# A fifth pair of hidden chunks by seven block products, two more tiles on written lists, and the output products chained in their banks

## The chip, the core and the metric

The kernel runs on one core of a Trainium2 chip. Its engines are TensorE (PE in the profile; its weight loads are the row PEld), VectorE (DVE), ScalarE (ACT), GpSimd (POOL) and SyncE (SP), which here only issues DMAs. Each engine takes its own instructions in order and waits for the others by semaphores. The metric is the device time of one execution in microseconds (us); a profiled execution gives the trace.

## What is computed

Blockwise causal attention over 8 batches of 8 heads, 576 positions and 64 dimensions, then a gated feed-forward layer over the 4608 tokens:

```python
batch, n_heads, seq, head_dim = (8, 8, 576, 64)
n_tokens, d_model, d_ff = (4608, 512, 1536)

scores = scale * np.matmul(q, k.transpose(0, 1, 3, 2))
mask = block_i >= block_j                    # blocks of 64 positions
scores = np.where(mask, scores, -1000000000.0)
attn = np.exp(scores - np.max(scores, axis=-1, keepdims=True))
attn = attn / (np.sum(attn, axis=-1, keepdims=True) + 1e-09)
x = np.matmul(attn, v).transpose(0, 2, 1, 3).reshape(B * S, H * D)

gate = np.maximum(x @ w_gate, 0.0)
val = x @ w_val
return (gate * val @ w_out).astype(np.float32)
```

## The kernel before

**Tiles.** The tokens are worked through in nine tiles of 512. Tile j (0 to 7) holds the first 512 positions of batch j; tile 8 holds the 64 last positions of all batches. While PE works on the feed-forward of tile j it also does the attention of batch j+1, so that the transposed attention output `xT` of the next tile is there when it begins. Tiles 7 and 8 have no attention beside them.

**Feed-forward of a tile.** The 1536 hidden columns are 12 chunks of 128. A plain chunk is eight matmuls that move 512 columns each (four for the gate, `g`, four for the value, `v`), a relu on ACT (`r`) and a product on DVE (`h`). The out-projection multiplies the 12 chunks of `hT` by `w_out`: plainly it is 48 matmuls of 512 columns.

**Seven block products.** Where two chunks are taken as a pair, gate and value of 256 hidden columns are made out of seven block products in place of eight (Strassen's scheme in Winograd's form): each product is four matmuls of 256 columns (L1348, in `times`), over sums of blocks of `xT` (`X1` to `X7`, L1154) and of the weights (`U..`, L950). The products land in three PSUM banks y, z and m. In the lists, `p15` is a matmul step of pair 1, product 5; the letters after it are the evacuation of a pair: `a`, `b`, `l` copy banks to SBUF on ACT (L1371, L1374, L1389), `r` is a relu on ACT, `s`, `m`, `y`, `z` are f32 additions (L1377, L1382, L1393, L1396; `s` on POOL where `ON_POOL` says so), `H` and `L` are the products that make the two halves of `hT` (L1401, L1415). Pair n is chunks 2n and 2n+1. Tiles 3 to 6 take four pairs so (1, 2, 3, 5) and four chunks plainly (0, 1, 8, 9), tiles 7 and 8 all six pairs, tiles 0 to 2 none.

**The out-projection by seven products** (L1033, in `seven_products`) is 84 matmuls of 256 columns over sums of `hT` (`s....`, L992 on DVE) and of `w_out` (`weight_sums`, `weight_differences`; the latter change `w_out` in place). Tiles 2 to 8 use it, tiles 0 and 1 are plain (L1265). `M5` is a step of two matmuls of product 5. Products 3 and 5 share bank y, 4 and 2 bank z; 1, 6 and 7 have a bank each. `oa`, `oy`, `oz` are ACT copies out of y and z (L1085, L1092, L1095); `ob`, `om`, `oc`, `od`, `o6`, `o7` are f32 additions (L1080; `od` on POOL). `S0` to `S3` store a quarter of the tile.

**What sets the order.** Tiles 3 to 8 follow lists (`ORDER_3_6`, `ORDER_7`, `ORDER_8`): each word emits a step, and each engine's queue holds its own instructions in the order of the words. Tiles 0 to 2 come from a generator of matmul steps (`ffn_gen`), into which the other work is put at places in a table (`AT`). Which of two or three PSUM banks a tile uses is written out too (`SLOTS`, `PAIR_BANK`). Attention in a list: `A` computes scores, `E` their exponentials (ACT, L616 and L623), `C` zeroes masked corners in `attnT` (L1526, eight memsets in a tile on DVE), `V` multiplies by v (L759, L773), `N` normalises (DVE), `T` transposes by DMA.

Of the kernel before, what the change touches and what calls it, by code (L numbers as in the profile page):

```python
# [10 lines left out]
FP = mybir.dt.float32  # L11
# [6 lines left out]
def kernel(  # L18
# [21 lines left out]
    SEVEN = 2  # L40
    PAIRS = (0, 2, 4, 6, 8, 10)
    OUT_2 = (3, "oa", 4, "ob", 1, "om", 5, "oy", 2, "oz", "S0", "oc", "od", 6, "o6", "S1", 7, "o7", "S2")
# [3 lines left out]
            "010101010101010010101010101010101010101010101010101010101001110010100110"  # L46
            "100111001010011010011100101001101001110010100110100110100101"
        ),
        "ffnp": (
            "021021021020210210210210210210120210120202010101210120201201120120210211"  # L50
            "201021102101020120120120121201202101202101202101210210201102220201101202"
            "001201202112000202112102022102102011022202011012020012012021120002021121"
            "0202210210122001201200121012012"
        ),
        "ob": (
            "043210432104310420312142324014203124304232410421302431423240142031243042"
            "324104210324103140231403"
        ),
        "gate_sb": (
            "021021021021021021021021021021021021021021011201201002102101120120100210"  # L60
            "21021021"
        ),
    }
    ORDER_3_6 = """
        A0 E0t X1 X3 X4 X6 Y4 g0 X7 E0u E0s C01 E0f g0 K g0*2 r0 k g1*2 v0*2 C00 l0 l1
        l2 v0 p15 v0 h0 p15 p1a g1*2 V00 U02 N00 r1 P V01 N01 p12*2 p1b p1s p13 l3 w0
        p13 p1r p11 v1*2 p11 l4 l5 p1m p14 p16*2 p1y d0 p14 p1l v1 U01 U06 U42 l6 l7 l8
        d1 d2 A1 E1u v1 h1 p17*2 p32 E1t E1s E1f p25*2 p32 g8 p1z p1L C11 p22*2 g8*2
        p35*2 C10 s0101 p1H s0112 p2a p23*2 p2b p24 p21 g8 p21 p24 p3b p2r p26 s0012 l9
        l10 d3 w1 p3a p3s s0001 p26 p2s p2m p2y p2H p33*2 p31*2 p3m p2l p27*2 p2z p3r  # L70
        p36*2 p3y r8 p34*2 p3l V11 N11 A2 E2t E2u E2f p2L p37*2 p3z U41 w2 w3 p52*2
        s1101 p55*2 s0212 p3L p5b v8*2 V10 N10 p51 v8*2 h8 p5a p53*2 p51 p54 p5s p5m E2s
        C21 g9*2 p54 s1201 p5r p56 g9 p56 g9 p5l p57 r9 p57 v9*4 p5y p5z C20 h9 M3*2 A3
        E3t p5L s2001 E3s p3H U45 s1012 s2101 s1112 s1001 E3u p5H s2112 U05 E3f U07
        s2012 V21 N21 C31 M4 M3*2 M4 M3*2 U46 U47 w4 w5 C30 V20 N20 M1*3 M4*3 T1 T0 oa
        M5 M1*2 M4 ob V31 M5 V30 M5 N31 M5*2 T2 N30 T3 M1 M5 M2*4 oy M2*2 S0 oz s0201
        s2212 s1212 S1 s2201 M6*2 om M7 M6*3 oc od M7 M6 M7*4 o6 S2 o7
    """
    ORDER_7 = """
        p15 p05 X1 p05 p0a p02*2 p0b p12*2 p1b p01 X3 X4 p03 p0s p03 p0r p15 p1a p04*2  # L80
        p0l p01 p1s X6 p06*2 p13*2 p1r p25*2 X7 p07*2 p0m p0y p0H Y1 p0z p0L p11 p22*2
        p11 P p2a p2b p2s p23*2 p2r p16 p14*2 p1l p16 p1m p1y p24 p26 p21*2 p26 s0101
        p24 p2l p1H p35*2 p3a p2m p2y p32*2 p27*2 p45 p3b p3s p45 p4a s0001 p2H p2z
        p17*2 p1z p33 p34 p33 p55 p42*2 p3r p34 p31*2 p2L p4b p4s p1L p3l p36*2 p55 p5a
        p3m p3y p3H s1101 p43*2 p4r p44 p37*2 p3z p3L s0112 p52 p41 p46 p52 p5b p41 p4m
        p53*2 p5r p5s p51 p44 p4l p51 p46 p4y p54 p47 p56 p54 p4H p5m p56 p5y p5l M4 p47
        p4z p57*2 p5z M3 M4 M3 M1 p5H M4*4 p4L p5L s1012 s1112 M3 s2112 s2101 M3*3 oa
        s0012 s1001 M1*5 M5 s2001 M5 s2012 M5*4 oy S0 ob M2*5 s0212 s0201 M6 s1201 s2212
        M2 M7 s1212 M6 s2201 oz S1 M6 M7 M6*3 om oc od o6 Y3 M7*4 o7 S2
    """  # L90
    ORDER_8 = """
        X6 p12*2 p1b p15*2 p1a p1s X7 p02*2 p0b p05*2 p14 p11*2 p13*2 p0a p0s p1m p01
        p03 p14 p01 p0m p03 p1r p16*2 p1y p1H p1l p17*2 p1z p0r p06*2 p04*2 P p0y p22*2
        p1L p0l p0H p2b s0112 p25*2 p32*2 p35 p07 p35 p2a p2s p07 p0z p0L p23*2 p3a p24
        p21*2 p2m p24 p2r p26*2 p3b p3s p2y p2H p55 p2l p33*2 p31 p34 p31 p34 p3r p36
        s0001 p3m p36 p3y p3H p55 p27*2 s0101 p2z p3l p37*2 p3z p52*2 p51 p5a p42 p45*2
        p5b p54 p53*2 p2L p3L p5s p42 s1001 p41 p4a p43 p41 p51 p43 p5r p56 p5m p56 p54
        p5y p4b p4s p44*2 p4m p5H p4r M3 p46*2 p5l p57 p4l p47*2 p57 M3 p4y p4z p5z M4*2
        p4H M4*3 p4L p5L M1 M4 M3*3 s1012 s1101 s2101 M3 s1112 M1 s2112 M1*3 oa s0012 M5
        s2001 M5 s2012 M5*4 ob oy S0 s2212 M2*5 M1 s0212 s2201 M2 oz S1 s1212 s0201  # L100
        s1201 M6*6 om oc o6 M7*6 S2 od o7b Sb o7a Sa
# [23 lines left out]
        (3, 1): ('sc', 'ffn', 'sc'),  # L125
        (3, 2): ('one', 'sc', 'ffn'),
        (3, 3): ('sc', 'ffn', 'ffn'),
        (3, 5): ('ffn', 'one', 'sc'),
        (4, 1): ('sc', 'ffn', 'sc'),
        (4, 2): ('one', 'sc', 'ffn'),  # L130
        (4, 3): ('sc', 'ffn', 'ffn'),
        (4, 5): ('ffn', 'one', 'sc'),
        (5, 1): ('sc', 'ffn', 'sc'),
        (5, 2): ('one', 'sc', 'ffn'),
        (5, 3): ('sc', 'ffn', 'ffn'),
        (5, 5): ('ffn', 'one', 'sc'),
        (6, 1): ('sc', 'ffn', 'sc'),
        (6, 2): ('one', 'sc', 'ffn'),
        (6, 3): ('sc', 'ffn', 'ffn'),
        (6, 5): ('ffn', 'one', 'sc'),  # L140
        (7, 0): ('one', 'sc', 'sc'),
        (7, 1): ('ffn', 'ffn', 'one'),
        (7, 2): ('ffn', 'sc', 'sc'),
        (7, 3): ('one', 'ffn', 'ffn'),
        (7, 4): ('sc', 'ffn', 'one'),
        (7, 5): ('sc', 'ffn', 'ffn'),
        (8, 0): ('sc', 'ffn', 'ffn'),
        (8, 1): ('ffn', 'one', 'sc'),
        (8, 2): ('sc', 'ffn', 'one'),
# [689 lines left out]
    def to_xT_dma(r):  # L839
# [1235 lines left out]
```

## Time and profile before

| | us |
|---|---|
| three runs | 348.38, 348.57, 348.59 (median 348.57) |
| profiled execution | 348.39 |
| its span, first to last instruction | 346.60 |

| stretch of the profiled execution | us | PE busy | DVE busy | ACT busy | POOL busy |
|---|---|---|---|---|---|
| start, loads, first attention | 0 to 20.00 | 17.37 | 13.23 | 13.15 | 11.14 |
| rest of tile 0 | 38.57 | 38.17 | 18.14 | 22.83 | 23.38 |
| tile 1 | 42.03 | 41.36 | 26.01 | 24.73 | 31.18 |
| tile 2 | 38.78 | 38.51 | 32.51 | 20.68 | 19.54 |

The stretches are cut where PE goes over from one tile's out-projection to the next tile. Busy time is the union of an engine's instructions; PE's is modelled, so the time between the starts of its matmuls is the better measure of what they cost.

### The profile page before, as it was taken

How to read it: one execution, taken by the hardware profiler on the slowest of the kernel's cores; microseconds unless marked ns; L12 is line 12 of the kernel's file. 1: busy time of each engine (PE TensorE's matmuls, PEld its weight loads, DVE VectorE, ACT ScalarE, POOL GpSimd, SP SyncE). 2: the span in 40 equal slices, each digit the busy share in tenths (PEclk: the TensorE clock that was granted, in tenths of full speed). 3: DMA queues.
4: the chain of work that ended last, by engine and by line, in shares of the span. 5: the costliest groups of instructions: out<-in, count | busy, mean ns of one | idle time of the engine just before them, and what ended most of it. 6: DMA issues, size and time to landing. Idle time of an engine off the chain costs nothing.

```text
span 346.6 us, 9051 instructions
## 1 busy us (share of the span) xinstructions
PE 334.8 (97%) x3481; PEld 233.9 (67%) x3518; DVE 273.0 (79%) x690; ACT 207.5 (60%) x341; POOL 194.7 (56%) x229
## 2 busy tenths in 40 slices
PE   8999999999999999999999999999999999999994
PEld 4544455545545559676977787778778788888873
DVE  4854455768629897789977997899899989999995
ACT  4942756587335872687468746884588537526721
POOL 2767566477795901986087627872155636612530
PEclk9999999999999999999999999999999999999999
DMA  8999999999999994999299929993400141012005
GB/s 244 294 352 373 360 217 242 229 155 176 184 218 113 137 191 82 190 174 139 40 158 181 152 40 156 164 171 47 121 32 2 33 129 33 2 41 83 3 0 121
DMA packets 155403, 50.07 MB, mean 144 GB/s; under 512 B 134464, under 2 KB 151744, under 8 KB 155360
## 3 DMA queue, kind: packets, MB, share of 16 engines
q1 hardware_dynamic: 77520, 32.52, 43.7%
q0 software_dynamic: 70528, 8.98, 43.3%
q10 hardware_dynamic: 7312, 8.00, 8.3%
q8 instruction: 27, 0.44, 0.5%
q14 instruction: 16, 0.13, 0.1%
HBM read 37.75 MB, written 9.44 MB: 136 GB/s over the span
## 4 chain that ended last, share of the span: by engine, by line
PE 75%; DMA 10%; DVE 9%; issue 2%; ACT 2%; POOL 1%; DVEq 0%; SPq 0%; ACTq 0%; POOLq 0%
PE ffnp L1033 11%; PE ffnp L1162 11%; PE ffnp L1348 9%; PE ffnp L1322 7%; PE sc L1348 7%; PE ffnp L1265 5%; PE one L1348 5%; PE one L1033 4%; PE sc L611 3%; DMA stage<-in_moe_w_out_dram 3%; PE ffnp L759 3%; DMA stage<-in_moe_w_val_dram 2%; DMA stage<-in_moe_w_gate_dram 2%; PE one L611 2%; DVE ob L1382 2%
## 5 line engine op out<-in xcount | busy, mean ns | idle before, releaser
L616 ACT ACTIVATE attnT<-sc 128x1024 bf16<-128x1024 f32 x56 | 56.3, 1037 | 0.0
L1033 PEld LDWEIGHTS <-stage 128*128 128x128 bf16 x420 | 39.9, 98 | 4.8 <-DVE stage L992 0.2
L992 DVE TENSOR_TENSOR stage<-hT 128x512 bf16<-128x512 bf16 (+2 forms) x120 | 39.6, 382 | 0.2
L1162 PE MATMUL ffnp<-xT,wg 128*128 128x512 bf16 x130 | 36.2, 379 | 0.6
L1172 ACT ACTIVATE gate_sb<-ffnp 128x512 bf16<-128x512 f32 x35 | 20.5, 598 | 27.0 <-PE ffnp L1162 22.7
L1080 POOL TENSOR_TENSOR ob<-ob,ob 128x512 f32<-128x512 f32 x7 | 8.9, 1268 | 45.7 <-DVE ob L1080 19.9
L1348 PEld LDWEIGHTS <-stage 128*128 128x128 bf16 x288 | 27.6, 98 | 7.4 <-issue 0.4
L759 PEld LDWEIGHTS <-attnT 128*128 128x128 bf16 x640 | 26.1, 98 | 9.2 <-DVE attnT L1526 1.1
L1033 PE MATMUL ffnp<-stage 128*128 128x256 bf16 x252 | 32.0, 273 | 0.0
L1162 PE MATMUL ffnp<-xT,wv 128*128 128x512 bf16 x108 | 31.3, 380 | 0.2
L1182 DVE TENSOR_TENSOR hT<-gate_sb,ffnp 128x512 bf16<-128x512 bf16 x28 | 19.1, 684 | 14.1 <-PE ffnp L1162 11.5
L623 ACT ACTIVATE attnT<-one 128x512 bf16<-128x512 f32 (+1 forms) x28 | 15.0, 536 | 22.2 <-PE ffnp L611 11.6
L489 POOL DMA_DIRECT2D v_bf<-in_v_dram x30 | 24.5, 826 | 3.5 <-PE sc L759 1.6
L1348 PEld LDWEIGHTS <-wg 128*128 128x128 bf16 x224 | 21.5, 98 | 5.7 <-issue 1.5
L1348 PEld LDWEIGHTS <-wv 128*128 128x128 bf16 x224 | 21.8, 98 | 4.1 <-DVE perm L1154 0.2
L1265 PE MATMUL ffnp<-wo,hT 128*128 128x512 bf16 x91 | 23.2, 379 | 0.3
L1162 PEld LDWEIGHTS <-wv 128*128 128x128 bf16 x144 | 12.9, 98 | 14.7 <-issue 1.8
L1162 PEld LDWEIGHTS <-wg 128*128 128x128 bf16 x144 | 13.4, 98 | 13.8 <-issue 0.5
L1401 POOL TENSOR_TENSOR hT<-gate_sb,ob 128x512 bf16<-128x512 bf16 x16 | 19.0, 1188 | 4.0 <-DVE ob L1393 3.9
L489 POOL DMA_DIRECT2D q_bf<-in_q_dram x20 | 18.0, 906 | 3.7 <-DVE recip L732 3.5
L611 PEld LDWEIGHTS <-kTm 64*128 64x128 bf16 x384 | 11.3, 94 | 12.9 <-issue 7.3
L1377 POOL TENSOR_TENSOR ob<-ob,ob 128x512 f32<-128x512 f32 x8 | 10.1, 1265 | 16.7 <-ACT ob L1371 10.2
(228 smaller groups left out, 911.7 us busy)
## 6 DMA issues: line engine op xcount, KB each, us to landing
out_dram<-ob ACTq DMA_DIRECT2D x28, 256.0 KB, 3.6
stage<-in_moe_w_val_dram SPq DMA_DIRECT2D x6, 512.0 KB, 8.7
stage<-in_moe_w_gate_dram SPq DMA_DIRECT2D x6, 512.0 KB, 8.3
stage<-in_moe_w_out_dram SPq DMA_DIRECT2D x6, 512.0 KB, 10.5
q_bf<-in_q_dram POOLq DMA_DIRECT2D x20, 128.0 KB, 4.8
k_bf<-in_k_dram POOLq DMA_DIRECT2D x20, 128.0 KB, 5.9
v_bf<-in_v_dram POOLq DMA_DIRECT2D x20, 128.0 KB, 6.3
stage<-in_v_dram SPq DMA_DIRECT2D x19, 128.0 KB, 5.4
```

The costliest lines, as they stand in the source:

```text
L489: ins = nc.gpsimd.dma_start(dst, part_of)
L611: nc.tensor.matmul(o, kTm[b % 2][head_of(hh), c, hp, :], qT, start=True, stop=True)
L616: return lambda: nc.scalar.activation(at[:, :, lo : lo + 512], sc, AF.Exp, scale=scale)
L759: nc.tensor.matmul(av[:, p, :], at[:, col : col + 128], v_bf[b % 2][:, c, h, :], start=(p == 0), stop=(c == p), skip_group_check=True,)
L992: nc.vector.tensor_tensor(out=out.rearrange("p (c n) -> p c n", c=m), in0=a, in1=b, op=op)
L1033: nc.tensor.matmul(to, sums.of(c)[which][:, 128 * p : 128 * p + 128], right, start=first, stop=(c == 5), skip_group_check=True,)
L1162: nc.tensor.matmul(to, (wg, wv)[t][f // 4][:, c, 128 * (f % 4) : 128 * (f % 4) + 128], x[:, c], start=(c == 0), stop=(c == 3),)
L1172: nc.scalar.activation(gate_sb, gate, AF.Relu)
L1182: nc.vector.tensor_tensor(out=h, in0=gate_sb, in1=val, op=AX.mult)
L1265: nc.tensor.matmul(op, hT[f][:, 128 * s : 128 * (s + 1)], wo[f // 4][:, f % 4, n0:n1], start=(f == 0), stop=(f == 11),)
L1322: nc.tensor.matmul(to, (wg, wv)[t][f // 4][:, c, 128 * (f % 4) : 128 * (f % 4) + 128], x[:, c], start=(c == 0), stop=(c == 3),)
L1348: nc.tensor.matmul(st[key][:, 256 * k : 256 * k + 256], left[:, c, 128 * k : 128 * k + 128], right[:, c], start=new and (k, c) == (0, 0), ...
```

## The change

Tiles 3 to 6 take a fifth pair, 4 (chunks 8 and 9), by seven products; chunks 0 and 1 stay plain. The block sums of the weights for pair 4, which were made in tile 6 for tile 7, are made in tile 2. Tiles 1 and 2 leave the generator: `ORDER_1` and `ORDER_2` emit them through `program(j)`, and tile 1's out-projection is done by seven products like tile 2's. Tile 0 keeps its order, now written as `ORDER_0`. In tiles 1 to 6 the out-projection's products are in another order: 5, 3, 6 accumulate one after the other in bank y and 2, 4, 7 in bank z, with copies between, which removes `oc` and `od`; one of the hidden differences gets the other sign for it. Six of the eight corner memsets of a tile go from DVE to POOL (four) and ACT (two copies of zeros). The weight differences are made in tile 1 instead of tile 2, some weight sums move between POOL and DVE, the block sums of x and of the weights lie in other buffers, and tile 1's stores are issued by SP. The lists of tiles 7 and 8 are new; their work is the same.

```diff
     ORDER_3_6 = """
-        A0 E0t X1 X3 X4 X6 Y4 g0 X7 E0u E0s C01 E0f g0 K g0*2 r0 k g1*2 v0*2 C00 l0 l1
...
-        s2212 s1212 S1 s2201 M6*2 om M7 M6*3 oc od M7 M6 M7*4 o6 S2 o7
+        X1 A0 E0t g0*3 P v0*2 X3 X4 X6 E0s E0u g0 r0 p15 v0 p15 p1a C01 v0 h0 l0 l1 l2
...
+        p4L p57*2 p5H l9 M2*2 p5z s0101 p5L M5*3 s2101 C20 E3t E3u E3s C31 l10 M1*2 V21
+        M1*2 s2112 M1 M5 M1 s2001 s2012 s2201 V20 N21 M5*2 N20 T2 U07 w3 C30 V30 N30
+        M2*2 oa ob M3*2 V31 N31 T3 om s1212 s0201 M3*4 M4 oy M4*5 oz S1 S0 M6*4 s2212 M6
+        M7 M6 U02 U01 M7*5 d3 o6 S2 w4 w5 o7 U06
     """
...
     ORDER_8 = """
...
-        s1201 M6*6 om oc o6 M7*6 S2 od o7b Sb o7a Sa
...
+        om oz S1 M7 M6 s2212 M7 oc od M7 M6 M7*2 o7b Sb o7a Sa M6*3 o6 S2
     """
...
+    ON_ACT = set(
+        """
+        1C10 1C11 1C31 2C01 2C11 2C30 2C31 3C20 3C30 4C20 4C30 5C20 5C30 6C20
+        6C30
+        """.split()
+    )
...
+    LAST_CHUNKS = {3: (1, 2, 0, 3, 5, 4), 4: (1, 2, 0, 3, 5, 4), 5: (1, 2, 0, 3, 5, 4), 6: (1, 2, 0, 3, 5, 4)}
...
-            (nc.sync if j == 2 else nc.scalar).dma_start(
+            (nc.sync if j <= 2 else nc.scalar).dma_start(
...
-                a, b = h[:, 2 * k0 : 2 * k1, 256:512], h[:, 2 * k0 : 2 * k1, 0:256]
-                op, m = AX.subtract, 2 * n
+                if self.j in OUT_34:
+                    nc.vector.tensor_tensor(
+                        out=out.rearrange("p (c n) -> p c n", c=2 * n),
+                        in0=h[:, 2 * k0 : 2 * k1, 256:512],
+                        in1=h[:, 2 * k0 : 2 * k1, 0:256],
+                        op=AX.subtract,
+                    )
+                    return
+                four = h[:, 2 * k0 : 2 * k1].rearrange("p (k c) (u n) -> p k (c u) n", c=2, u=2)
+                a, b, op = four[:, :, 1:3], four[:, :, 0:4:3], AX.subtract
...
+        def products(which):
+            key = {5: "y", 3: "y", 6: "y", 2: "z", 4: "z", 7: "z", 1: "m"}[which]
+            new = which in (5, 2, 1)
+            if new:
+                st[key] = bank(OUT_BANK.get((j, key), {"z": "one"}.get(key, "ffn")))
+            steps = [(p, c) for c in range(0, 6, 2) for p in range(2)]
...
+            for p, i in steps:
+                for c in chunks[i : i + 2]:
+                    times(half(st[key], p), which, p, c, new and (p, c) == (0, chunks[0]))
+                yield
...
+            elif name == "om":
+                add("", st["g"], st["m"], st["g"], AX.subtract)
...
+            elif name == "o6":
+                st["c22"] = ob()
+                add("", st["c22"], st["y"], st["g"], AX.add)
+            elif name == "o7":
+                add("", st["g"], st["z"], st["g"], AX.add)
...
+        return (products_34, do_34) if j in OUT_34 else (products, do)
...
+    def zero_act(o):
+        two = zeros[64:128, 0:256].rearrange("p (g c n) -> p g c n", g=2, c=2)
+        nc.scalar.copy(o.bitcast(FP), two.bitcast(FP))
...
-        for j in range(3, B + 1):
+        for j in range(1, B + 1):
             do, end = program(j)
```

`OUT_34` is `[7, 8]`: these two tiles keep the old out-projection (`products_34`, `do_34`). The removed names are those of the generator for tiles 1 and 2, the table `AT`, `outs` and `OUT_2`.

## The prediction

> **What bounds the kernel now.** I read first the busy time of each engine in stretches cut at the tiles: after the colon the length, then PE, PEld, DVE, ACT and POOL with their instructions in brackets, granted clock, DMA share, GB/s.
>
> ```profile
> 139.38:175.40 36.02, 35.53 (x414) 27.64 (x420) 31.40 (x83) 24.15 (x40) 22.75 (x25) 1.00 1.34 141
> 175.40:211.59 36.19, 35.81 (x415) 27.56 (x420) 31.30 (x82) 24.12 (x40) 22.04 (x25) 1.00 1.25 135
> 211.59:247.52 35.93, 35.57 (x414) 27.63 (x420) 31.37 (x82) 24.16 (x40) 22.12 (x25) 1.00 1.30 132
> 247.52:283.44 35.92, 35.56 (x414) 27.85 (x419) 32.67 (x85) 24.14 (x40) 17.91 (x16) 1.00 0.18 47
> 283.44:312.47 29.03, 28.49 (x255) 24.27 (x253) 27.59 (x56) 14.56 (x27) 13.76 (x12) 1.00 0.12 38
> 312.47:341.90 29.43, 28.40 (x252) 23.95 (x250) 28.03 (x55) 14.99 (x27) 10.53 (x10) 1.00 0.12 33
> ```
>
> These are tiles 3 to 8. PE is busy nearly throughout. In tiles 3 to 5 DVE is at 87% (31.40 of 36.02), in tile 6 at 91%, in tiles 7 and 8 at 95%. A busy PE is not yet a full one, so I took the spacing of matmuls from the chain that ended last (start, length, what):
>
> ```profile
> 91.27 1.73 PE ffnp L1265 x8
> 172.78 2.62 PE ffnp L1033 x24
> 180.34 0.45 PE ffnp L1348 x4
> 180.81 0.59 ACT ob L1374
> 181.43 0.70 DVE ob L1377
> ```
>
> Eight plain matmuls of 512 columns take 1.73 us, 216 ns each; 24 of 256 columns take 2.62 us, 109 ns each. Tile 7 is 6 x 28 + 84 = 252 matmuls of 256 columns, 27.5 us at 109 ns; it lasted 29.03, so PE lost 1.5 us there, and 1.9 in tile 8. The named waits of PE say where it lost time elsewhere (total, times, longest):
>
> ```profile
> PE one L1517 <- DVE zeros L211: 1.0, 1, 1.0
> PE one L1033 <- POOL hT L1401: 0.6, 1, 0.6
> PE sc L611 <- DVE ob L1393: 0.3, 1, 0.3
> ```
>
> The first is the start, the second tile 8, the third tile 3. So tiles 1 to 6 are bound by the matmuls themselves, tiles 7 and 8 by DVE, which PE then waits for.
>
> **The change part by part.** *The fifth pair.* Two plain chunks are 16 matmuls of 512 columns: 16 x 216.5 ns = 3.46 us. Seven products are 28 of 256: 28 x 109.2 = 3.06. PE saves 0.41 us a tile, 1.62 in tiles 3 to 6. *Tile 1's out-projection:* 48 x 216.5 ns = 10.39 becomes 84 x 109.2 = 9.17, saving 1.22. PE's work falls by 2.84 us, all of it in tiles where PE is the bound.
>
> The Trainium skill speaks against this: its page "TensorE: Matmul & The Clock Gate", section "Back-to-back issue gap", gives about 131 ns a matmul at 512 columns and 81 at 128 for a stream of loads and matmuls in a real kernel, so that narrow matmuls cost more than their share. Taking 98 ns for 256 between these (an estimate from that page), the pair would cost 28 x 98 - 16 x 131 = 0.65 us more and the whole PE term would be +4.5 us. The rows above, 216 and 109 ns in this very stream, refute that here.
>
> *What the pair costs elsewhere, per tile of 3 to 6.* DVE gains the pair's `m`, `y`, `z`, `s`, one `H` (32H moves there) and `L`, at 0.69 (L1382), 0.69 (L1393), 0.68 (L1396), 0.69 (L1377), 0.68 (L1401 on DVE) and 0.68 (L1415): 4.1 us. It loses two products of plain chunks (2 x 0.68, L1445), `oc` (0.69, L1080) and six corner memsets (6 x 0.165, L1526): 3.05. Net +1.06. ACT gains three copies (3 x 0.60) and two corner copies, loses one relu (0.60). Such a corner copy (64 partitions, 128 words) is not in the trace; the nearest rows are an ACT copy of 128 elements, 0.27, and one of 256, 0.37; I take 0.27, so ACT has +1.7 on 24.1 of 36, which leaves a quarter free. POOL loses `od` (1.27) and gains four corner memsets (4 x 0.307, the row L1529): nothing net, and DVE no longer waits for `od` (2.1 us of its idle time in tile 3).
>
> So DVE is at 32.5 of 35.6 us in tiles 3 to 5, 91%, and in tile 6, where one block sum (0.5) moves on to tile 7, at 33.2 of 35.5, 94%. No row shows what this makes PE wait. From below it is nothing (a queue with 9% free, spread well, is never late); from above it is the 1.5 to 1.9 us a tile that PE lost at 95%. I take 0.1 each for tiles 3 to 5 and 0.4 for tile 6, nearer the lower end, because the work is spread more evenly: counted by the row durations over eight equal parts of a tile's matmuls (4.5 us), the fullest part had 6.8 us of DVE work and has 5.5. That is +0.7. The cover is that slack; if it is gone, the upper end is rival B. One more bound belongs here: the differences with the changed sign read a new pattern, six a tile. The row for such a sum is 0.415 (L992, 512 elements); if the pattern lost that speed it would be that of f32, 0.687, +1.6 us of DVE a tile. Their inner runs stay 256 elements as before, so I take nothing.
>
> *Chained banks.* In tiles 1 to 6 product 3 may begin only when `oa` has copied y, 6 only after `oy`, 4 after `ob`, 7 after `oz`. Behind a waiting matmul stands all of PE. The tightest place in tiles 3 to 6 is product 5, `oa`, product 3: from the start of the last `M5` matmul PE has 0.11 + V30 (15 x 30 ns) + two `M2` steps (4 x 0.109) = 1.00 us. Before, tile 8 has the same pattern with 0.98 us, eight matmuls of product 1 from 335.16:
>
> ```profile
> 335.16 1.10 PE L1033 MATMUL ffnp<-stage 128*128 128x256 bf16 x8
> 335.36 0.59 ACT L1085 COPY ob<-ffnp 128x512 f32<-128x512 f32 x1 [4.60 <-PE ffnp L1033]
> 336.10 1.47 PE L1033 MATMUL ffnp<-wo,stage 128*128 128x256 bf16 x12
> ```
>
> The eight need 0.87 us, the next began 0.94 after them: 0.07 lost. At 1.00 us it is 0.05 a tile; tiles 1 and 2 have three places at 0.98. Sum 4 x 0.05 + 3 x 0.07 = +0.4, if ACT is free at that moment; the last exponentials (`E3`) stand well ahead of `oa` in its queue. If it is not, rival C.
>
> *Tiles 1 and 2.* DVE takes over in tile 1 twelve hidden sums (about 5.8 by L992), the twelve differences (12 x 0.28, L915), and two groups of weight sums; corners leave: +9 on 26.0 of 42.0, still 86%. Tile 2 is relieved by 6 (the differences, three block sums of weights, three of x). POOL has eight block sums more in tile 2 (8 x 1.18, L950) on 19.5 of 38.8. SP takes tile 1's stores, ACT loses four DMA issues; a store lands in 3.6 us and nothing reads it. All nothing: hidden under PE, which has 40.5 and 38.2 us there. If a block sum were late, tile 3's first products would stand; their words come 10 us before.
>
> *Tiles 7, 8 and the end.* Their work is the same, but for one `s` (0.69) that goes to POOL in tile 8. The last bank is now product 6, so the end is `o6` (0.68) and a 128 KB store by SP and POOL in place of two halves (0.75 together) and 64 KB stores:
>
> ```profile
> 340.59 1.30 DVE ob L1080 x2
> 341.98 0.42 DVE ob L1080
> ```
>
> Stores of 128 KB by POOL take 2.6 us, 64 KB ones 2.3 to 2.5: +0.1. What the new order does to the 3.4 us lost in these tiles I can't read from rows; bounds -1.2 (tile 8's visible wait of 0.65 and as much again) and +1.0; I take 0.
>
> **Sum.** -2.84 + 0.7 + 0.4 + 0.1 = -1.64 on the profiled execution's 348.39 (span 346.60 and 1.79 around it): 346.75. The median of the runs is 348.57, 0.18 above that execution; the forecast for a median lies between, and I round to 346.7.
>
> **The rivals.** *A, the waits go too:* no new wait in tiles 3 to 6 (0.7 + 0.4 not paid) and up to 1.2 won in tiles 7 and 8: 348.39 - 2.84 - 0.6 to -1.2, 344.4 to 345.6, centre 345.0. For it: DVE loses its wait for `od`. Against: DVE stays at 95% in tiles 7 and 8. *B, slower: DVE becomes the bound of tiles 3 to 6.* Place: the evacuations of the five pairs; it decides once DVE passes some 95% of a tile, which 1.6 us more (slow differences) would bring. Price: tile 7's 1.5 us in each of four tiles, less the 0.3 now lost: +5.7 - 2.84 + 0.4 = +3.3, 351.6; at half of it 348.8. For it: tiles 7 and 8. Against: 9% free. *C, the copies between chained products come late:* an exponential of 1.04 us (L616) ahead of `oa` in four tiles and half of one in tiles 1 and 2: +5 at worst, +2.4 likely; 348.39 - 2.84 + 0.7 + 2.4 = 348.6. *D, it doesn't do what it says:* narrow matmuls that cost more than half of wide ones. By rows, 12 more weight loads of 98 ns uncovered would be +1.2 us a pair, 353 in all; the 24 in 2.62 us show them covered. The rule of the Trainium skill weighed above would end on this side too.
>
> **How the numbers follow.** Forecast 0.50 (345.6 to 347.8), A 0.22, B 0.12, C 0.14, D 0.02. About 0.2%, 0.7 us, is what a measurement of this kernel tells from no change. Faster: forecast, A and a quarter of C, 0.75. Same (347.9 to 349.3): half of C and a third of B, 0.11. Slower: the rest, 0.14. The range takes in A and C and the lighter B: 344.6 to 349.0; the likeliest case's own is 345.6 to 347.8.
>
> **What would show it.** Right: tiles 3 to 5 last 35.6 to 35.9 us, tile 1 about 1.2 less, DVE at 91% there; differences (L992's successor) at 0.415. Wrong: PE's waits list DVE or ACT tiles with some tenths each in every tile (B: pair sums; C: copies before products 3, 6, 7), or tiles 7 and 8 change by over 1 us.

## The result, and the profile after

| | us |
|---|---|
| the kernel before, beside it | 348.38 to 348.60, median 348.58 (4 executions) |
| the changed kernel | 357.44, 359.14, 359.90, 360.95, median 359.52 |
| ratio | 1.0311, interval 1.0258 to 1.0363 |
| profiled execution of the changed kernel | 359.14, span 357.36 |

The change makes the kernel slower by 10.9 us. The changed kernel also scatters over 3.5 us where the kernel before scattered over 0.2. The windows of the changed kernel, cut where PE goes over to the next tile (tiles 1 to 8 in order; length, then busy time of PE, PEld, DVE, ACT and POOL with instructions in brackets, granted clock, DMA share, GB/s):

```profile
57.06:102.28 45.22, 43.94 (x526) 27.03 (x524) 38.26 (x94) 28.12 (x47) 35.12 (x44) 1.00 1.25 161
102.28:147.15 44.87, 41.35 (x425) 24.68 (x425) 31.13 (x79) 22.77 (x39) 22.35 (x24) 0.96 1.15 131
147.15:185.70 38.55, 36.35 (x428) 28.62 (x428) 31.84 (x80) 25.25 (x44) 22.58 (x27) 1.00 1.48 136
185.70:221.73 36.03, 35.60 (x432) 28.68 (x429) 31.80 (x80) 25.80 (x45) 22.53 (x27) 1.00 1.33 136
221.73:257.80 36.07, 35.59 (x433) 28.73 (x429) 31.71 (x80) 25.80 (x45) 22.49 (x27) 1.00 1.30 128
257.80:292.96 35.16, 34.74 (x416) 28.32 (x413) 31.79 (x81) 25.46 (x44) 12.33 (x13) 1.00 0.20 52
292.96:323.12 30.16, 28.40 (x254) 24.37 (x252) 28.75 (x57) 14.85 (x27) 13.82 (x11) 1.00 0.11 37
323.12:357.36 34.24, 28.44 (x254) 24.27 (x251) 28.33 (x57) 14.58 (x27) 12.11 (x11) 0.96 0.20 56
```

The kernel before is cut in the same way, by the first up-projection matmul of each tile (56.93, 100.53, 140.08, 176.10, 212.29, 248.21, 283.28 and 312.31 us). So cut, its tile 1 lasts 43.60 us; the 42.03 of the table ahead of the prediction begins 1.64 us later, inside that tile. Its tiles 1 and 2:

```profile
56.93:100.53 43.60, 42.88 (x480) 23.07 (x489) 27.06 (x72) 25.73 (x41) 31.73 (x40) 1.00 1.51 184
100.53:140.08 39.55, 39.28 (x421) 24.25 (x424) 32.64 (x95) 21.09 (x34) 20.31 (x26) 1.00 1.34 148
```

The prediction's column adds up its terms tile by tile:

| | before | after | change | predicted change |
|---|---|---|---|---|
| up to tile 1 | 56.93 | 57.06 | +0.13 | 0 |
| tile 1 | 43.60 | 45.22 | +1.62 | -1.1 |
| tile 2 | 39.55 | 44.87 | +5.32 | +0.1 |
| tile 3 | 36.02 | 38.55 | +2.53 | -0.26 |
| tile 4 | 36.19 | 36.03 | -0.16 | -0.26 |
| tile 5 | 35.92 | 36.07 | +0.15 | -0.26 |
| tile 6 | 35.07 | 35.16 | +0.09 | +0.04 |
| tile 7 | 29.03 | 30.16 | +1.13 | 0 |
| tile 8 to the end | 34.29 | 34.24 | -0.05 | +0.1 |

The loss lies in tiles 1, 2, 3 and 7. The fifth pair, in tiles 3 to 6, brings next to nothing but costs little either. The waits of PE name what it stood for (total, times, longest):

```profile
PE ffnp L1375 <- DMA xT<-xnat: 3.7, 4, 2.3
PE ffnp L1375 <- DVE hT L1499: 1.4, 2, 0.8
PE sc L662 <- DVE ob L1449: 1.2, 4, 0.3
PE one L1571 <- DVE zeros L262: 1.0, 1, 1.0
PE sc L1401 <- DVE ob L1435: 0.9, 1, 0.9
PE one L1401 <- ACT ob L1424: 0.9, 1, 0.9
```

L1375 are plain matmuls, L1401 those of a pair, L662 the scores; L1571 is the start, as before. The first line is new: in the kernel before PE never stood for the transposed attention output `xT`. The timeline of the changed kernel around the start of tile 2 (start, length, what):

```profile
96.35 5.99 SPq L893 DMA_TRANSPOSE xT<-xnat  x4
102.52 1.42 SPq L550 DMA_TRANSPOSE qTm<-q_bf  x1
...
102.28 0.39 PE L1375 MATMUL ffnp<-xT,wv 128*128 128x512 bf16 x1 [0.27 <-DMA xT<-xnat]
...
105.82 1.87 PE L1375 MATMUL ffnp<-xT,wg 128*128 128x512 bf16 x4 [2.29 <-DMA xT<-xnat]
```

All four transposes of tile 2 are issued from 96.35 on. In the kernel before, the first was issued at 84.53 and the last at 94.58 (it had landed by 101.08, though its transposes took 6.5 to 8.9 us to land beside loads and stores):

```profile
84.53 11.95 SPq L842 DMA_TRANSPOSE xT<-xnat  x4
```

The list of tile 1 says why. In it `@a8` and `@b8` make the two halves of round 8's product with v and normalise them, and `@x8` issues its transpose; `@d` issues transposes of q and k, `@l` loads, `@t` belongs to the 64 last positions (`@td` are its casts), `@W` and `@D` are weight sums and differences. The words `@x11 @x9 @x8` put two transposes whose inputs were normalised by 89.6 us behind one whose input was ready at 96.3, and a queue goes in order. PE then works off the few matmuls that need only the first blocks, stands 2.29 us, and what follows runs at a granted clock of 0.50 (the third column from the end):

```profile
102.28:105.82 3.54, 1.25 (x6) 0.49 (x6) 0.84 (x2) 0.32 (x1) 0.00 (x0) 0.99 1.17 145
105.82:109.19 3.37, 3.37 (x9) 1.14 (x9) 0.00 (x0) 1.19 (x2) 0.00 (x0) 0.50 1.15 259
109.19:113.00 3.81, 3.81 (x19) 1.77 (x18) 1.07 (x2) 1.19 (x2) 0.00 (x0) 1.00 0.58 156
```

At 0.50 for 3.37 us this is another 1.7 us lost. With the waits for `xT` (2.6) and for a hidden product (0.6) that is 4.9 of the 5.32 us that tile 2 lost.

### The profile page after: what moved, and what is told of

Its sections match the earlier page's. It is cut to its first block, busy times and chain, and to the rows that moved or that the text cites. A ratio compares the mean times of both kernels' runs of the same rounds, so it can differ in the third digit from the quotient of the medians.

```text
span 357.4 us, 9274 instructions
## 1 busy us (share of the span) xinstructions
PE 339.2 (95%) x3602; PEld 243.0 (68%) x3602; DVE 283.8 (79%) x681; ACT 217.2 (61%) x367; POOL 197.1 (55%) x241
## 5 line engine op out<-in xcount | busy, mean ns | idle before, releaser
L1073 PEld LDWEIGHTS <-stage 128*128 128x128 bf16 x480 | 45.5, 98 | 6.3 <-issue 0.2
L1370 ACT ACTIVATE gate_sb<-ffnp 128x512 bf16<-128x512 f32 x43 | 25.7, 605 | 27.1 <-PE ffnp L1375 18.6
L1375 PE MATMUL ffnp<-xT,wg 128*128 128x512 bf16 x124 | 36.7, 390 | 4.3 <-DMA xT<-xnat 3.4
L1401 PEld LDWEIGHTS <-stage 128*128 128x128 bf16 x360 | 34.6, 98 | 9.1 <-issue 2.2
L1375 PE MATMUL ffnp<-xT,wv 128*128 128x512 bf16 x116 | 33.7, 382 | 1.1 <-DVE hT L1499 0.8
L1030 DVE TENSOR_TENSOR stage<-hT 128x512 bf16<-128x512 bf16 (+2 forms) x88 | 31.1, 393 | 0.3
L1073 PE MATMUL ffnp<-stage 128*128 128x256 bf16 x216 | 29.8, 273 | 0.0
L1401 PEld LDWEIGHTS <-wg 128*128 128x128 bf16 x256 | 24.2, 98 | 7.2 <-issue 3.2
L1401 PEld LDWEIGHTS <-wv 128*128 128x128 bf16 x256 | 24.4, 98 | 5.0 <-issue 2.1
L1375 PEld LDWEIGHTS <-wg 128*128 128x128 bf16 x128 | 12.1, 99 | 17.1 <-issue 6.4
L1499 DVE TENSOR_TENSOR hT<-gate_sb,ffnp 128x512 bf16<-128x512 bf16 x29 | 19.6, 683 | 3.2 <-PE ffnp L1375 2.0
L662 PEld LDWEIGHTS <-kTm 64*128 64x128 bf16 x384 | 11.4, 94 | 14.7 <-issue 10.3
L1073 PEld LDWEIGHTS <-hT 128*128 128x128 bf16 x192 | 18.0, 98 | 3.8 <-POOL hT L1454 1.2
L1375 PEld LDWEIGHTS <-wv 128*128 128x128 bf16 x128 | 11.9, 99 | 12.7 <-issue 3.4
L1430 POOL TENSOR_TENSOR ob<-ob,k_bf 128x512 f32<-128x512 f32 x9 | 12.2, 1358 | 14.6 <-ACT ob L1424 7.2
L662 PE MATMUL sc<-qTm,kTm 64*128 64x512 bf16 (+1 forms) x168 | 18.3, 306 | 1.7 <-DVE ob L1449 1.2
```

The source lines that it names most:

```text
L662: nc.tensor.matmul(o, kTm[b % 2][head_of(hh), c, hp, :], qT, start=True, stop=True)
L1030: nc.vector.tensor_tensor(out=out.rearrange("p (c n) -> p c n", c=m), in0=a, in1=b, op=op)
L1073: nc.tensor.matmul(to, sums.of(c)[which][:, 128 * p : 128 * p + 128], right, start=first, stop=(c == (5 if j in OUT_34 else chunks[-1])), ...
L1370: nc.scalar.activation(st[key], of, AF.Relu)
L1375: nc.tensor.matmul(to, (wg, wv)[t][f // 4][:, c, 128 * (f % 4) : 128 * (f % 4) + 128], x[:, c], start=(c == 0), stop=(c == 3),)
L1401: nc.tensor.matmul(st[key][:, 256 * k : 256 * k + 256], left[:, c, 128 * k : 128 * k + 128], right[:, c], start=new and (k, c) == (0, 0), ...
```

## The experiments

Each is the changed kernel with words of its lists moved (or, where said, an engine changed); what is computed stays the same. 4 builds on 3, each of 5 to 9 on the one before it, 10 to 12 on 9. Times are medians of four executions, with the kernel before beside them at 348.3 to 348.6. Tile lengths are from one profile each, cut as above.

| kernel | median | ratio, interval | tile 1 | 2 | 3 | 4 | 5 | 6 | 7 |
|---|---|---|---|---|---|---|---|---|---|
| changed | 359.52 | 1.0311, 1.0258-1.0363 | 45.22 | 44.87 | 38.55 | 36.03 | 36.07 | 35.16 | 30.16 |
| 1 x8, x9 first | 358.83 | 1.0288, 1.0251-1.0325 | 46.21 | 43.03 | 38.63 | 36.02 | 36.07 | 35.16 | 30.28 |
| 2 x12, d4 first | 358.79 | 1.0294, 1.0252-1.0336 | 45.31 | 44.44 | 37.53 | 36.03 | 36.06 | 35.17 | 30.15 |
| 3 both | 355.77 | 1.0201, 1.0160-1.0242 | 48.54 | 41.72 | 36.02 | 36.04 | 36.05 | 35.16 | 30.28 |
| 4 x9 behind t2 | 354.77 | 1.0179, 1.0133-1.0224 | 45.12 | 42.01 | 36.85 | 36.04 | 36.06 | 35.17 | 30.16 |
| 5 scores, X7 | 361.06 | 1.0365, 1.0326-1.0404 | 46.31 | 41.52 | 38.69 | 37.72 | 38.01 | 36.84 | 29.20 |
| 6 sums on VectorE | 360.29 | 1.0346, 1.0302-1.0390 | 47.88 | 40.35 | 39.93 | 37.72 | 38.02 | 36.84 | 29.20 |
| 7 tile 1's order | 360.39 | 1.0338, 1.0315-1.0360 | 46.13 | 40.49 | 38.42 | 37.72 | 38.03 | 36.84 | 29.20 |
| 8 scores back | 352.90 | 1.0119, 1.0085-1.0153 | 45.66 | 40.42 | 38.17 | 36.02 | 36.06 | 35.16 | 29.19 |
| 9 stores earlier | 351.92 | 1.0103, 1.0077-1.0129 | 44.82 | 41.03 | 36.02 | 36.03 | 36.06 | 35.17 | 29.19 |
| 10 A2 alone | 355.26 | 1.0213, 1.0171-1.0255 | 44.52 | 40.35 | 38.77 | 36.56 | 36.59 | 35.68 | 29.19 |
| 11 all W on VectorE | 356.64 | 1.0237, 1.0220-1.0253 | 45.24 | 40.26 | 40.31 | 36.03 | 36.08 | 35.16 | 29.20 |
| 12 loads earlier | 360.23 | 1.0339, 1.0321-1.0356 | 44.73 | 48.78 | 36.03 | 36.03 | 36.05 | 35.17 | 29.20 |

Tiles 4 to 7 repeat within 0.1 us, so one profile settles a term there. Tile 1 scatters by 3 us and tile 2 by 1; there a single length proves little, and the waits and single instructions have to be read. Part of that scatter is the granted clock: in the profiles of kernels 3 and 6 it stood at 0.50 for 3.41 us inside tile 1, which costs 1.7 us. The timeline of kernel 3 cut there:

```profile
62.87:66.28 3.41, 1.79 (x48) 1.15 (x47) 2.92 (x5) 0.90 (x3) 3.41 (x5) 1.00 1.03 228
66.28:69.69 3.41, 3.41 (x21) 1.76 (x21) 1.40 (x3) 2.15 (x4) 3.41 (x5) 0.50 1.35 223
```

In the first stretch PE stood 1.62 us for tile 1's first hidden product. In kernel 5 it stood as long at the same place (PE busy 1.79 us from 63.26 to 66.67) and the clock stayed at 1.00.

### The order of SyncE's queue (1, 2, 3, 4)

```diff
-        ... @b8 ... @b9 ... @a11 @b11 M3*2 @x11 @x9 @x8 M3*4      (ORDER_1; 1 and 3)
+        ... @b8 @x8 ... @b9 @x9 ... @x11 M3*4
-        @a12 g9 ... @b13 g9*2 ... s2001 @d4 @x12      (ORDER_2; 2 and 3)
+        @a12 @x12 g9 ... @b13 @d4 g9*2 ... s2001
-        @b9 @x9 ... M5 @t2 s2212      (4, on top of 3)
+        @b9 ... M5 @t2 @x9 s2212
```

> Against the changed kernel (359.5, profiled 359.1). Theory Q, the order of SyncE's queue: two transposes that are ready at about 88 to 90 us stand behind one whose input is ready at 96.3, so all four of tile 2's xT land late. Moved ahead, the two late ones are issued at about 96.4 and 99.7 and land by 103.5: tile 2's wait for xT falls from 2.3 to 0 to 1.0 us, the granted clock stays 1.00 in tile 2, tile 2 lasts 40 to 42 us instead of 44.9, and the loads that wait for its first hidden products come earlier too: 354 to 356 in all. Rival D, VectorE is too late in tile 1 (its normalising at 96 and 99 us sets the end whatever the queue does): within 0.7 of 359.1. Rival C, the copies between chained products set the end of tile 1: the same, within 0.7.

> Only tile 2's list: the first xT transpose of tile 3 right behind its attention, and the four q and k transposes of batch 4 two places earlier. Theory Q: tile 2 still starts late (2.3 us of wait and the lower clock), but tile 3's two waits for xT (0.64 and 0.45) go, so tile 2 and 3 together last 1 to 2 us less: 357.3 to 358.3. Rival D: tile 3 is late because VectorE and ScalarE are, no change (within 0.5 of 359.1).

> Both moves. Theory Q: the sum of the two, 353 to 355, tile 2 at 40 to 42 us and tile 3 at 36.5 to 37.5, no wait for xT above 0.5 us. What is left above the 348.6 of the kernel before then lies in tile 1 (some 3 us of small waits for VectorE), in the scores of tiles 4 to 6 (0.6 us a tile) and in tile 7 (1 us). Rivals D and C: within 0.7 of 359.1.

> As the kernel with both moves (355.8; profiled 356.7), but the second early transpose behind the tail transposes qTt, kTt of batch 2, which it had held up (PE waited 1.0 us for qTt there). Theory Q: tile 3 again 36.0 us, tile 2 41 to 42, tile 1 some 1 us shorter than the 48.5 of that profile, 354 to 355.5. Rival: tile 1's length is set by something else (it was 45.2, 46.2, 45.3 and 48.5 us in four profiles with the same work), the total stays within 0.5 of 355.8.

What each move was to cure is gone: in 1 the granted clock is 1.00 in the first 10 us of tile 2 and the 2.3 us of wait are gone (1.4 us for `xT` in tile 3 stay); in 3 PE's list has no wait for `xT` at all, and tile 3 is at 36.02, the length that it had before the change. The totals are weaker evidence. Those of 1 and 2 (358.8 both) miss the theory's numbers and lie inside the bounds of their rivals; in 1 tile 1 took up part of the gain. That of 3, 355.8 for 353 to 355, does not: its executions (354.1 to 356.7) lie clear of the changed kernel's (357.4 to 361.0), and the rivals, which asked for 359.1, are out as the main cause. What 3 lost in tile 1 was the hidden product and the clock shown above, and partly its own doing: x9, still being normalised, held up `qTt` and `kTt` of batch 2, for which PE then waited 0.4 us and its weight loads 0.6. The total of 4, 354.8, is inside its 354 to 355.5, but its executions overlap with those of 3, so its 1.0 us is not shown. The order of one queue, in these two places, cost about 4 us.

Tile 1's stores were a suspect too, and were put back on ScalarE:

```diff
-            (nc.sync if j <= 2 else nc.scalar).dma_start(
+            (nc.sync if j == 2 else nc.scalar).dma_start(
```

> Only tile 1's stores back on ScalarE. On SyncE they are issued last, at 110.75 us, behind all of the transposes, and nothing reads them before the buffers come round: theory Q expects nothing (359.1 within 1). If these stores held up the later transposes or the ob buffers (rival S), the time falls by 1 us or more.

Its executions took 357.79, 360.94, 364.76 and 366.88 us; with that scatter it shows no gain, and its total tells nothing more.

### GpSimd holds up VectorE (5, 6, 7, 11)

```diff
-        p05*2 p0a X1 X3 X4 X6 p12*2 ... p1a p1s X7 p03*2      (ORDER_7; 5)
+        p05*2 p0a X1 X3 X4 X6 X7 p12*2 ... p1a p1s p03*2
-        p37 p3z A2 E2t E2u p4s p44*2 p41*2 ... M2 A3 E3f p4L p57*2      (ORDER_3_6; 5)
+        p37 p3z p4s p44*2 A2 E2t E2u p41*2 ... M2 p4L p57*2 A3 E3f
-        U07 U15 U16 U21 U22 U42 U45 U47 U57 W1 W2 W3 W5      (ON_POOL; 6: U42, U47; 7: W5)
+        U07 U15 U16 U21 U22 U45 U57 W1 W2 W3
-        @W0 @W1 @td1 h0 ... @u1q @D1 g4*3 ... v5*2 @D3      (ORDER_1; 7)
+        @W0 @W1 h0 @td1 ... @u1q g4*3 ... v5*2 @D1 @D3
```

> As the last, with three words moved: the scores A2 and A3 of tiles 3 to 6 two matmul steps later, and in tile 7 the block sum X7 directly behind X6. Theory B (banks): A2 and A3 each stand 0.3 us for the score bank that an evacuation still reads, so tiles 4 and 5 fall from 36.05 to 35.4 to 35.6 us. Theory P (GpSimd holds up VectorE): in tile 7 X7 (512 bf16 from SBUF) started 0.04 us after an addition on GpSimd of 1.28 us and took 1.52 us in place of 0.42, and PE then waited 0.92 us; ahead of it X7 takes 0.42, the wait goes and tile 7 falls from 30.2 to 29.1 to 29.4 us. Rival D (VectorE is simply full in tile 7, at 95%): the order of its words matters little, tile 7 stays at 29.9 to 30.3. Sum under B and P: 3 us less than the last kernel.

> As the last, with the two block sums of weights U47 and U42 of tile 2 on VectorE instead of GpSimd. VectorE gets 2 x 0.42 us more work. Theory P: in tile 2 three VectorE sums took 1.21, 1.23 and 1.05 us in place of 0.42, 0.68 and 0.42 while GpSimd made these two, the next hidden product was late by that and PE waited 1.05 us; so tile 2 falls by 0.6 to 1.1 us. Rival D: more work on VectorE makes tile 2 longer, 0 to 0.8 us.

> As the last, with tile 1's VectorE order changed: the casts td1 behind the first hidden product h0 (PE waited 0.8 to 2.1 us for it), the weight difference D1 next to D3 (it ran at 71.8 us beside a GpSimd cast, 2.17 us for two instructions of 0.29), the weight sum W5 on VectorE (0.71 us; on GpSimd it held up two sums, 1.44 in place of 0.75). Theory P with the order of VectorE's queue: tile 1 falls by 1 to 3 us, to 43 to 45. Rival: tile 1's length is set by transfers (loads and transposes of batches 2 and 3), no change beyond its scatter of 3 us.

The clearest place is the start of tile 7. The timeline of the changed kernel, and behind it that of kernel 9, where X7 stands behind X6:

```profile
295.79 1.28 POOL L1430 TENSOR_TENSOR ob<-ob,k_bf 128x512 f32<-128x512 f32 x1 [3.37 <-ACT ob L1424]
295.83 1.52 DVE L1255 TENSOR_TENSOR perm<-xT 128x512 bf16<-128x512 bf16 x1
297.27 0.68 DVE L1435 TENSOR_TENSOR ob<-sc,ob 128x512 f32<-128x512 f32 x1
298.00 0.60 PE L1401 MATMUL sc<-xT,stage 128*128 128x256 bf16 x4 [0.92 <-DVE ob L1435]
```

```profile
286.88 1.75 DVE L1255 TENSOR_TENSOR perm<-xT 128x512 bf16<-128x512 bf16 x5
288.55 0.68 DVE L1430 TENSOR_TENSOR ob<-ob,k_bf 128x512 f32<-128x512 f32 x1
```

A block sum takes 0.42 us; five of them, partly overlapped, 1.75. The one that began 0.04 us after GpSimd's addition ended 0.28 after it and took 1.52. The evacuation behind it was late, and PE stood 0.92 us. Moved by one word, tile 7 lasts 29.20 in place of 30.16, in every later kernel too. VectorE is as full as before (27.67 of 29.19 us, 95%), so the rival (fullness) is out. How near it was shows in the profile of the kernel with tile 1's stores on ScalarE, where X7 is not moved. There GpSimd and VectorE began within 0.01 us of each other, the sum was done in 0.42, the addition took 1.57, PE did not stand, and tile 7 lasted 29.03 (that execution was the slowest of its four, but its tiles 4 to 6 are as long as in the others):

```profile
304.64 1.57 POOL L1430 TENSOR_TENSOR ob<-ob,k_bf 128x512 f32<-128x512 f32 x1 [3.37 <-ACT ob L1424]
304.65 0.42 DVE L1255 TENSOR_TENSOR perm<-xT 128x512 bf16<-128x512 bf16 x1
```

So the old order left to a few hundredths of a microsecond which of the two had to wait. The Trainium skill, page "SBUF — State Buffer", section "SBUF: two separate sides", says that VectorE and GpSimd share a pair of SBUF ports which the one that starts first holds for its whole instruction, where the VectorE instruction has two SBUF inputs or runs in a two-port mode. The rows of this sum, which reads two blocks in SBUF, agree.

The same happens in tile 2, to which the change brought block sums of weights on GpSimd. The timeline of kernel 3:

```profile
130.47 1.20 POOL L992 TENSOR_TENSOR wg<-wg,wv 128x512 bf16<-128x512 bf16 x1
131.00 1.23 DVE L1030 TENSOR_TENSOR stage<-hT 128x1024 bf16<-128x1024 bf16 x1
131.59 1.65 POOL L992 TENSOR_TENSOR stage<-wv 128x512 bf16<-128x512 bf16 x1
132.47 1.05 DVE L1030 TENSOR_TENSOR stage<-hT 128x512 bf16<-128x512 bf16 x1
133.44 0.67 DVE L1499 TENSOR_TENSOR hT<-gate_sb,ffnp 128x512 bf16<-128x512 bf16 x1
134.17 0.81 PE L1375 MATMUL ffnp<-xT,wg 128*128 128x512 bf16 x3 [1.05 <-DVE hT L1499]
```

Undisturbed, the two L1030 take 0.68 and 0.42; the hidden product L1499 was late by that, and PE waited. A third sum of VectorE, at 128.93 in kernel 3, took 1.21 in place of 0.42 with no computation on GpSimd: beside it GpSimd was issuing three loads (128.35 to 130.48). With the two sums on VectorE (kernel 6) this wait is gone, with more work on VectorE, and tile 2 is 1.17 us shorter than in kernel 5 (0.6 to 1.1 were expected). That is no more than one profile's scatter, but tile 2 stays at 40.3 to 41.0 in kernels 7 to 11 and was 41.5 to 42.0 in 3 to 5. But tile 3 grew by 1.24: what it then waited for is told below.

In tile 1 the same is seen in single instructions, again in the changed kernel:

```profile
61.55 0.64 DVE L397 CAST k_bt<-stage 64x256 bf16<-64x256 f32 x1
62.22 1.13 DVE L404 CAST v_bf<-stage 64x256 bf16<-64x256 f32 x1
63.38 0.69 DVE L1499 TENSOR_TENSOR hT<-gate_sb,ffnp 128x512 bf16<-128x512 bf16 x1
...
71.79 2.17 DVE L957 TENSOR_TENSOR wo<-wo 128x256 bf16<-128x256 bf16 x2
```

The casts take 0.28 and 0.37 at their shortest in this profile and a difference (L957) 0.28. Beside GpSimd's sums and casts they took up to four times that. Summed over tile 1, VectorE's instructions were 5.4 us longer than the shortest of the same line and shape in the profile (1.1 in the kernel before). The first hidden product stood behind the two casts, and PE 0.78 us for it (2.1 in the profile of kernel 1). In kernel 7 the differences take 0.28 again, but tile 1, at 46.13, missed its 43 to 45: it is 1.8 shorter than in kernel 6, of which 1.7 is the clock that fell there, and the same as in kernel 5. PE's wait of 1.6 us for the first hidden product had become one of 1.3 for the second, which stood behind the same casts. Kernel 11, on top of 9, put the weight sums W1, W2 and W3 on VectorE as well:

> As the one with the earlier stores, and the weight sums W1, W2 and W3 of tile 1 on VectorE as well, so that GpSimd makes none there. VectorE's own work grows by 3 x 0.71 us. Theory P (GpSimd's sums hold up VectorE's): VectorE's instructions in tile 1, 5.6 us longer than their undisturbed durations in the changed kernel, are so by 3 us or less, and tile 1 does not grow (0 to -1.5 us). Rival D (VectorE's own work sets tile 1): tile 1 grows by 1 to 2 us.

Tile 1 did not shrink (45.24 against 44.82), and the excess did not either (3.9 us against 3.3 in kernel 9). So GpSimd's weight sums are not what keeps tile 1 long; its other casts and copies, and the loads that it issues, remain untested. What is left there is 2.4 us (44.82 against 43.60 less the 1.22 to be saved), in many waits of 0.1 to 0.6 us. The total of 11 is 4.7 us above that of 9 mostly for another reason, in tile 3 (40.31 against 36.02): a wait of 2.4 us that comes up again below, and the clock at 0.50 for 3.41 us behind it.

### The scores' bank (5, 8, 10)

Tiles 4 and 5 lack the 0.41 us that the fifth pair saves. PE's time outside attention did fall, from 28.61 to 28.34 in tile 5; its stretches of attention matmuls grew from 7.31 to 7.73. The timeline of the changed kernel, at A2 in tile 5:

```profile
238.17 0.60 PE L1401 MATMUL sc<-perm,wg 128*128 128x256 bf16 x4
238.88 0.69 DVE L1449 TENSOR_TENSOR ob<-sc,ob 128x512 f32<-128x512 f32 x1
239.62 0.40 PE L662 MATMUL sc<-qTm,kTm 64*128 64x384 bf16 x4 [0.30 <-DVE ob L1449]
```

The scores go into the bank (`sc`) that the pair's last product has just filled, and stand until it is evacuated; A3 does the same (its last six matmuls, at 245.09, take 0.91 us where A1's take 0.60). Kernel 5 moved both later and lost 1.7 to 1.9 us a tile. The waits of PE in kernel 5:

```profile
PE ffnp L1401 <- ACT ob L1442: 3.6, 4, 0.9
...
PE sc L1073 <- ACT attnT L667: 1.4, 4, 0.4
PE sc L1401 <- ACT attnT L667: 1.3, 4, 0.3
```

The wait for the bank is gone, and a larger one for ScalarE has come: its exponentials start later, and the copies behind them too. Kernel 8 put the scores back (and in tile 1 `@td1` behind `@t0`): 352.9 us for 352 to 353.5, though tile 1, at 45.66, lies among the rival's 45.5 to 47. Kernel 10 moved A2 alone and gave ScalarE the next copy first:

```diff
-        p3z A2 E2t E2u p4s p44*2 p41*2 E2s p3L p52*2 p4l s1101
+        p3z p4s p44*2 p4l A2 E2t E2u p41*2 E2s p3L p52*2 s1101
```

> The scores A2 and A3 back in their places (moving them made tiles 3 to 6 some 1.7 us longer each, PE stood for ScalarE's copies), the other moves kept: transposes, X7, U47 and U42 on VectorE, D1 next to D3, W5 on VectorE; in tile 1 the casts td1 now behind both first hidden products (PE had waited 1.3 us for the second). Theory: tiles 4 to 6 again 36.04, 36.06 and 35.17 us, tile 7 29.2, tile 2 40.3 to 40.8, tile 1 44 to 45.5: 352 to 353.5 in all. Rival (tile 1 is set by transfers): tile 1 at 45.5 to 47, 354 or more.

> As the last, with A2 alone behind p44*2 in tiles 3 to 6 and the copy p4l ahead of its exponentials. Theory B: the 0.3 us that A2 stands for its bank goes and ScalarE is not later than before: 0.3 us a tile, 1.2 in all. Rival A (ScalarE's order is tight there): PE waits for the exponentials or for p4l instead, no gain or up to 1.7 us a tile more.

Rival A held: 0.5 us a tile more. ScalarE is busy 72% of a tile here and yet has no slack at this place.

### The loads behind the transposes (9, 12)

In tile 3 ScalarE's copy out of pair 1 waited for a store to land, and PE for the copy. The store was in SyncE's queue behind the transposes of `xT`, these behind those of q and k; in kernel 8 q's took 11.0 us to land beside GpSimd's loads of v, and SyncE stood 5.75 us issuing k's. Kernel 9 moved the store words, kernel 12 the loads as well:

```diff
-        ... h0 r1 h1 ... oy M4*4 oz M6*6 o6 U57 U11 U16 S1 P M7*3 U36 S2 S0 M7*3 o7      (ORDER_2; 9)
+        ... h0 P r1 h1 ... oy S0 M4*4 oz S1 M6*6 o6 U57 U11 U16 M7*3 U36 S2 M7*3 o7
-        v2 U52 g2*2 ... v3*4 @l4 U25      (12, on top of 9)
+        v2 U52 @l4 g2*2 ... v3*4 U25
```

> As the last, and tile 2's words for its stores earlier: the last store of tile 1 after the first hidden product, S0 and S1 directly behind the copies that they store. In tile 3 ScalarE's copy out of pair 1 waited 1.6 us for a store to land that SyncE had issued behind the transposes, and PE waited 0.4 to 0.9 us for that copy. Theory Q: this wait goes, tile 3 is 36.0 us instead of 36.9, the total 0.5 to 1 us less. Rival: the stores stand behind the transposes of tile 3 whatever the order of the words, no change.

> As the kernel with the earlier stores (351.9), and the loads of batch 4's q and k on GpSimd at the start of tile 2, behind tile 1's last hidden product instead of tile 2's third. They were issued from 113 us (before: 107.6, seven us into tile 2), and SyncE's queue then stood up to 8 us in the transposes of k, with the last xT transposes and tile 2's stores behind it; ScalarE waited up to 3 us for such a store. Theory Q (one late link after the other in SyncE's queue): with the loads 8 to 10 us earlier the queue is done 4 us sooner, tile 3 lasts 36.0 us in every profile, tile 2 40 to 41, no wait for an output buffer: 350.5 to 351.5. Rival (transfers compete for the DMA engines): the loads slow tile 1's last transposes, tile 2 starts later, no gain.

Kernel 9 is the best that was found, 351.92, still 1.0% slower than the kernel before. It is 1.0 us below kernel 8, with executions that overlap. Its tile 3 is 36.02, but kernel 10, with the same order there, has 38.77 and a wait of 1.6 us for the same copy, kernel 11 one of 2.4: the gain of the store words is not certain. Kernel 12 missed by far, and the rival held. Two of PE's waits, both in tile 2:

```profile
PE ffnp L1375 <- DMA xT<-xnat: 3.9, 1, 3.9
PE one L662 <- DMA kTm<-k_bf: 2.1, 1, 2.1
```

The last two transposes of tile 2 were issued at 96.1 and 99.3, no later than in kernel 9, but GpSimd's loads for batch 4 had begun at 94.4, and they took 8.8 and 7.2 us to land; in the changed kernel the four took 2.5 to 4.7. After each wait the clock stood at 0.50 for 3.41 us (from 107.81 and from 118.05); the waits (6.0 us) and the clock (up to 3.4) cover the 7.75 us by which tile 2 is longer than in kernel 9. Tile 3, on the other hand, was 36.03: its own transposes had no load beside them (2.4 us each).

Two more kernels on top of 12 moved small things:

```diff
-        v0*3 g1 g0 @td0 @x7 v1*3 ... s2212 s1202 C30 C31
+        v0*3 g1 g0 @x7 @td0 v1*3 ... s2212 C30 C31 s1202
-        p43 p4b p43 p37 p4r p37 p3z A2 ... M2 p56*2 p5y M2 A3      (second kernel)
+        p43 p37 p4b p37 p43 p4r p3z A2 ... p56*2 p5y M2*2 A3
```

> As the last, with two words moved in tile 1: the casts td0 behind the evacuation of x7 (PE waited 0.2 to 0.6 us for it) and two corner memsets ahead of a block sum (PE waited 0.4). Theory (order of VectorE's queue): 0.4 to 0.8 us less in tile 1. Rival: the wait moves to the next instruction, within 0.3.

> As the last, with the bank that A2 and A3 wait for in tiles 3 to 6 emptied sooner: p37 one step ahead of p43, and both steps of M2 between p5y and A3; nothing on ScalarE is moved in its queue. Theory B: each of the two waits of 0.3 us shrinks by 0.2, so 0.3 to 0.4 us a tile and 1.2 to 1.6 in all. Rival A: the relu p4r, now later, delays the exponentials and PE waits for these: no gain, or up to 0.5 us a tile more as when A2 was moved.

They took 363.81 and 364.93 us, because `kTm` landed yet later (PE waited 5.1 and 6.9 us for it) and the clock stood at 0.50 for 13.7 and 10.2 us of tile 2; tile 1 was 46.8 and 46.3, no shorter. In the second, A2's wait fell from 0.30 to 0.20 us, and tiles 4 to 6 grew by 0.15: again what the bank gave, the next wait took.

## Why the prediction was wrong

**The step that failed** is "*Tiles 1 and 2*", which put their edits at nothing: "All nothing: hidden under PE, which has 40.5 and 38.2 us there." Of the 12.4 us between 346.7 and 359.1, 10.7 lie in tiles 1, 2 and 3. The step counted busy time against PE's time. It followed SyncE only for the stores, and not for the `@x` and `@d` words, whose order the new lists set: two ready transposes behind a late one. That, with the clock that fell after it, was about 4 us (kernel 3). Moving words, and three sums to another engine, won back 7.6 us in all (kernel 9). "If a block sum were late, tile 3's first products would stand" looked at the wrong reader: the sums were not late, they made VectorE late, and the next hidden product with it (1.1 us in tile 2, kernel 6).

**PE's terms.** The pair's saving is there in PE's time outside attention (0.27 of 0.41), and the spacing of 109 ns held; rival D is out. Tile 1's 1.22 never showed as time, since tile 1 came to wait by more than that (+1.62). Kernel 9's profile is still 3.1 us longer than that of the kernel before, of which 1.2 lie in tile 1 and 1.5 in tile 2; why these wait in many small pieces is not settled.

**Waits in tiles 3 to 6.** I took 0.1 us a tile for a full VectorE. VectorE was at 88% (31.80 of 36.03), less than my 91, and was not the bound; rival B is out. The wait that came was of 0.3 us twice a tile, for a bank, at the scores. Term and mechanism were both off, though the size was small: tiles 4 to 6 together came out at +0.08 where -0.48 was forecast.

**The differences** (L1030) took 0.416 us, as taken. **Chained banks:** no wait for `oa`, `oy` or `ob` is in PE's list; +0.4 was too much, and rival C is out. **Tail:** tile 8 and the end changed by -0.05 for +0.1.

**Tile 7** was put at 0 with bounds of -1.2 and +1.0, as nothing could be read for it. It was +1.13, and 0.96 of it was one word; a few hundredths of a microsecond decided that: of the six profiles with this order of tile 7 five have 30.15 to 30.28 and one has 29.03.

**The range** had no case for the mechanism that decided, a queue that issues DMAs.

## What to carry to other kernels

Where a change reorders a list, write down for each queue that issues transfers what stands behind what and when each becomes ready, SyncE's and GpSimd's too: a transfer that is ready and stands behind one that is not is late by the whole difference, and what waits for it is late next. When work goes from VectorE to GpSimd, look at what VectorE does beside it; a sum moved there to relieve VectorE can hold it up for longer than the sum took. Costs of a stage that is "hidden under PE" must be checked by what each matmul waits for, not by busy shares. With a wait of PE goes what the granted clock may add: here 1.7 us behind waits of 1.6 and 2.3 us, in some executions and not in others.

## What the runs showed of the hardware

- An addition in SBUF on VectorE, begun while GpSimd computed, ended only after it: 1.52 us in place of 0.42 beside an instruction of 1.28. In all 17 traces, 232 VectorE instructions are 0.15 us or more longer than the shortest of their line and shape. None of them reads PSUM (evacuations such as L1435 and L1499 kept their 0.68 beside GpSimd's work), and each overlaps GpSimd's work: 201 a computation, 31 only the issue of a load.
- A DMA transpose of `xT` landed 2.4 to 2.5 us after its issue with nothing beside it, and 7.2 to 8.8 us with GpSimd's loads in flight (6.5 to 8.9 in the kernel before, where they were issued early enough).
- The granted clock fell to 0.50 for 3.37 us after PE had stood 2.29 us. The Trainium skill, page "TensorE: Matmul & The Clock Gate", section "What's actually happening", gives one window of about 3.4 us; the length agrees. Within each trace the moments at which the clock changes lie whole multiples of 3.41 us apart (in kernel 12: 107.81, 111.23, 118.05, 121.47). Cut on that raster up to the last matmul (and PE busy as the profile models it), every stretch at the full clock with PE busy under 40% was followed by 0.50 (8 in the 17 traces; here 1.16 of 3.41 us, 34%), none with PE busy over 56% was, and between 48% and 56% both happened. So the wait need not fill a stretch, and the same wait of 1.6 us cost 1.7 us more in kernel 3 and nothing more in kernel 5.
- The changed kernel's executions scatter by 3.5 us. The fastest, 357.44, has a mean granted clock of 0.998, the three others 0.992 or 0.993; one fall for 3.41 us is worth 0.005 and 1.7 us, so one fall fewer fits about half of the scatter. No run isolated the rest.
